# A 7x7 FFT convolution on one core: the weight copy first in the queue, the pixels behind it

## Chip, core and metric

The kernel runs on one core of one Trainium2 chip. The metric is the device time of one execution in microseconds (us). The kernel before was timed in three runs: 267.62, 270.09 and 271.57 us, median 270.09 us.

## What is computed

The reference takes an image x (1 x 224 x 224 x 96, bf16) and weights w (7 x 7 x 96 x 96, bf16), and multiplies them in the frequency domain:

```python
wp = jnp.pad(w, ((0, H - K), (0, W - K), (0, 0), (0, 0)))
Xf = jnp.fft.rfft2(x.astype(jnp.float32), axes=(1, 2))
Wf = jnp.fft.rfft2(wp.astype(jnp.float32), axes=(0, 1))
Yf = jnp.einsum('bhwi,hwio->bhwo', Xf, Wf)
y  = jnp.fft.irfft2(Yf, s=(H, W), axes=(1, 2)).astype(jnp.bfloat16)
```

The result is the cyclic 7x7 convolution of the image over 96 input and 96 output channels.

## The kernel before, in words

**Vertical direction: short transforms.** The 224 rows are cut into 8 blocks of 28 output rows (NJ, B), each seen through a window that is transformed to 17 frequencies (NS). Frequencies 0 and 16 are real, the other 15 complex, and a complex product is done with three real ones, so that each complex frequency has three weight planes ("slots"), the third being the difference of the first two (`diff`, line 390).

**Horizontal direction: taps.** The 7 horizontal taps are kept as taps, in a short fast-convolution scheme with 10 products per pair of pixels (NTAP, TAPS). The 224 columns are cut into 7 tiles t of 32 pixels.

**The stages, tile by tile.** In stage A, pixels of one image column (118 rows on the partitions: 112 rows of half an image and 6 rows of padding) are the stationary operand and the transform matrix Fm the moving one; the result goes through a PSUM bank to the buffer xf, on ScalarE or VectorE, whichever has the smaller sum of costs so far (`evac`, line 132). In stage B (`b_round`, line 556) there is one round per tile and frequency: TensorE multiplies xf and its sums and differences J (`jit`, line 526, on VectorE) by the weight planes WF, VectorE and ScalarE combine the products, and the result goes to a scratch in DRAM. Stage C transforms back with the matrix G and writes the output.

**The weights' own transform (the head).** The weights arrive as 49 rows (7 x 7 taps) of 96 x 96 numbers and have to be multiplied by the matrix Em to give WF. There are two jobs for this. The *wide jobs* (line 397) make the first 11 slots, enough for frequencies 0 to 4, in 24 jobs of four matmuls each, and read one copy of the weights, which holds all 96 output channels. The *prep jobs* (line 415) make the other slots in groups of three frequencies (PGRP) during the rounds, and read two copies of the weights at once: the second copy is shifted by 48 output channels, so that one matmul serves two channels. Both copies and Em lie in the tile wq; the first copy is at partitions 30 to 78 (W1 = 30), the second at 79 to 127, and the unused partitions 0 to 29 are zeroed, since wide jobs read partitions 0 to 78 and prep jobs all 128.

**The first two tiles are done out of order.** Tiles 0 and 1 run interleaved, tile 1 four rounds behind (LAG). Stage A of both is cut by frequency into three parts (SH2: frequencies 0 to 7, 8 to 12, 13 to 16) and by half image into two (`f_jobs`, line 511; `fj[part][half]`). A job covers 8 pixels or, in the third part, 16, and its matmuls are 64, 40 or 32 columns wide. Before, all three parts of the first half image of tile 0 are run ahead of the wide jobs (line 761); the second half's first part and the halo pixels (the six columns to the left, `a_bank`) run in the middle of the wide jobs (WMID), and J of rounds 0 to 2 is issued after the wide job 20 (JIT0). The second half's parts 1 and 2 are fillers between rounds (lines 823 and 824).

**What sets the order.** Each engine runs its instructions in program order. Fillers are put between the two halves of a round by the counter k: `add(a, b, jobs)` spreads a list of jobs over the steps a to b, two steps to a round as long as one tile runs and while both do (`pace`, line 786). The first prep jobs begin at k = 4, in the middle of round 2 (line 806). All loads and stores go through the queue of SyncE (SP), in order. Each uses one of eight semaphores in turn, so that the ninth DMA is not issued before the first has landed, and so on. Short matmuls on zeros (`warm`, line 218) keep TensorE busy while it waits for data: 14 at the start, FILL ahead of the wide jobs, one after every fourth of them.

**Constants.** Fm, Em and G are worked out on the chip: GpSimd (POOL) makes index patterns and masks (`mf` for Fm, `mk2` for Em), VectorE and ScalarE (a sine) the factors, and POOL the whole of G (`build_g`, line 340), finished by one sine and one product (`g_fin`) just ahead of round 0.

## Time and profile before

| what | value |
|---|---|
| three runs | 267.62, 270.09, 271.57 us |
| profiled execution, its own time | 269.31 us |
| its span in the profile | 267.5 us |
| TensorE (PE) busy | 255.1 us, 95% |
| VectorE (DVE) busy | 216.2 us, 81% |
| ScalarE (ACT) busy | 197.6 us, 74% |
| GpSimd (POOL) busy | 97.7 us, 37% |
| mean granted TensorE clock | 0.995 |

The span is what the profiler covers of the execution; 1.8 us of the execution's own time lie around it. All later times are counted from the start of the span. A row of the timeline gives the start, how long it lasts, engine, line, operation, the tiles written and read, the number of instructions merged into it, and in brackets the engine's idle time just before it with what ended it. PEld is the loading of the stationary operand, SPq the issue of DMAs. A row of the table of windows gives, for a stretch of time, its length, the busy time of PE, PEld, DVE, ACT and POOL (with the number of instructions that began), the granted clock, the share of time that the 16 DMA engines are busy, and GB/s.

### The profile page before, as it was taken

To read this page: it belongs to the slowest core of one execution; us is meant where nothing else is said; L and a number is where in the kernel's file an instruction comes from. 1 tells how busy PE (TensorE), PEld (TensorE's weight loads), DVE (VectorE), ACT (ScalarE), POOL (GpSimd) and SP (SyncE) were. 2 spreads that over 40 slices of the span, in tenths; PEclk is the share of its full clock that TensorE was granted. 3 is DMA by queue.
4 is the path that set the end of the run, shared out by engine and by line. 5 is a ranking of instruction groups with operands and counts; after the bars stand their busy time and mean duration, and the time that the engine had idled before them with its cause. 6 is when DMAs were issued, how large, how long until landed. Compare 5 with 4: busy or idle time off the path is not lost. (4 is left out here: it accounts for less than half of the span.)

```text
span 267.5 us, 12139 instructions
## 1 busy us (share of the span) xinstructions
PE 255.1 (95%) x5128; PEld 235.7 (88%) x5128; DVE 216.2 (81%) x465; ACT 197.6 (74%) x485; POOL 97.7 (37%) x152
## 2 busy tenths in 40 slices
PE   8897999999999999999999999999999999999983
PEld 2787999999998999999999998989999889879861
DVE  7997699889899788778887888778888789978523
ACT  8796978497964578998988789886988864187123
POOL 7771324364558344222222322233123323422100
PEclk9999999999999999999999999999999999999998
DMA  8994102711111697987876486979678443887845
GB/s 197 230 251 76 48 2 67 245 45 48 47 48 49 192 258 159 294 238 223 272 195 188 117 235 221 253 216 341 235 152 242 169 128 125 204 250 182 259 107 191
DMA packets 46690, 46.78 MB, mean 175 GB/s; under 512 B 35292, under 2 KB 38056, under 8 KB 46540
## 3 DMA queue, kind: packets, MB, share of 16 engines
q1 hardware_dynamic: 44348, 43.95, 59.6%
q10 hardware_dynamic: 2288, 2.06, 2.6%
q8 instruction: 40, 0.66, 1.1%
q14 instruction: 14, 0.11, 0.2%
HBM read 24.66 MB, written 21.33 MB: 172 GB/s over the span
## 5 line engine op out<-in xcount | busy, mean ns | idle before, releaser
L101 PE MATMUL pb<-WF,J 96*128 96x96 bf16 x2821 | 162.9, 206 | 1.7 <-DVE J L101 1.3
L101 PEld LDWEIGHTS <-J 96*128 96x128 bf16 x2821 | 138.0, 98 | 12.3 <-issue 3.5
L101 POOL TENSOR_TENSOR yf<-v,u 128x384 bf16<-128x384 f32 x79 | 81.3, 1040 | 145.7 <-issue 84.6
L101 ACT CAST xf<-pb 96x408 bf16<-96x408 f32 (+3 forms) x145 | 67.3, 486 | 7.6 <-PE pb L101 3.8
L101 PE MATMUL pb<-WF,xf 96*128 96x96 bf16 x952 | 60.0, 206 | 0.9 <-ACT WF L101 0.9
L101 DVE TENSOR_TENSOR J<-xf 96x1824 bf16<-96x1824 bf16 (+1 forms) x84 | 56.9, 716 | 0.0
L101 PEld LDWEIGHTS <-xf 96*128 96x128 bf16 x952 | 47.2, 98 | 1.3 <-issue 1.2
L101 PE MATMUL pb<-Fm,xn 118*128 118x136 bf16 (+3 forms) x640 | 45.5, 199 | 0.2 <-DVE u L101 0.2
L101 PE MATMUL pb<-tt,Gm 102*84 102x384 bf16 (+1 forms) x132 | 32.9, 326 | 0.6 <-ACT J L101 0.3
L101 PEld LDWEIGHTS <-xn 118*128 118x128 bf16 x640 | 30.3, 97 | 0.3 <-issue 0.3
L101 ACT CAST WF<-pb 96x480 bf16<-96x480 f32 (+1 forms) x58 | 28.6, 558 | 2.3 <-PE pb L101 2.3
L101 ACT CAST J<-pb 84x384 bf16<-84x384 f32 (+1 forms) x65 | 28.1, 490 | 2.6 <-PE pb L101 2.6
L101 ACT CAST yo<-pb 84x384 bf16<-84x384 f32 (+1 forms) x63 | 27.1, 486 | 2.3 <-POOL yf L101 1.3
L101 DVE TENSOR_TENSOR J<-J 96x912 bf16<-96x912 bf16 (+2 forms) x42 | 24.2, 576 | 0.0
L101 PE MATMUL pb<-wq 128*128 128x120 bf16 (+1 forms) x288 | 21.8, 226 | 0.7 <-DMA wq<-in_w_dram 0.6
L101 PEld LDWEIGHTS <-wq 128*128 128x128 bf16 (+1 forms) x288 | 19.9, 148 | 1.7 <-DVE xf L101 1.1
L101 DVE TENSOR_TENSOR yf<-v,u 128x384 bf16<-128x384 f32 x26 | 15.1, 580 | 0.9
L101 PE MATMUL pb<-wu 128*112 128x384 bf16 (+1 forms) x59 | 14.5, 391 | 1.1 <-DVE ct L101 1.1
L101 PEld LDWEIGHTS <-wu 128*112 128x112 bf16 (+1 forms) x59 | 7.4, 127 | 5.6 <-issue 3.1
L101 PEld LDWEIGHTS <-Gm 102*84 102x84 bf16 (+1 forms) x132 | 11.1, 117 | 1.0 <-issue 0.4
L101 ACT COPY xf<-xf 96x816 bf16<-96x816 bf16 (+3 forms) x20 | 11.1, 613 | 0.0
L101 ACT CAST tt<-pb 112x384 bf16<-112x384 f32 x8 | 3.6, 480 | 9.3 <-PE pb L101 9.2
(387 smaller groups left out, 239.2 us busy)
## 6 DMA issues: line engine op xcount, KB each, us to landing
scr<-yf SPq DMA_DIRECT2D x30, 288.0 KB
xn<-in_x_dram SPq DMA_DIRECT2D x12, 672.0 KB
tt<-scr SPq DMA_DIRECT2D x24, 336.0 KB
out_dram<-yo SPq DMA_DIRECT2D x12, 252.0 KB
out_dram<-J SPq DMA_DIRECT2D x12, 252.0 KB
tt<-scr SPq DMA_DIRECT2D x6, 288.0 KB
WF<-in_x_dram SPq DMA_DIRECT2D x2, 672.0 KB
out_dram<-tt SPq DMA_DIRECT2D x8, 168.0 KB
```

The costliest lines, as they stand in the source:

```text
L101: r = fn(*a, **k)
```

## The change

The change concerns the head and the first rounds; the rounds' own matmuls are the same.

- **Order of the loads.** The first weight copy is issued first, then the pixels of tile 0 (first half image), where it was the other way round.
- **Places.** The first copy goes to partitions 64 to 112 (W1 = 64), the second to 15 to 63 (W2 = 15); 15 rows are zeroed instead of 30. The wide jobs read only the 49 rows of the first copy, and 110 columns of Em instead of 128.
- **Order on PE.** 15 warm matmuls (before: 14, and 3 more behind the first pixels), then the wide jobs; part 0 of the first half image ahead of wide job 12, the halo ahead of wide job 18, part 0 of the second half after the last, then two warm matmuls, J and round 0.
- **Moved to the rounds.** Parts 1 and 2 of the first half image of tile 0 become fillers with those of the second half: part 1 over the steps 1 to 6, part 2 over 6 to 10. `diff` of frequencies 2 to 4 is one step later. The copy of tile 0's edge columns to tile 1 (`new_xf`) is issued at round 2 instead of round 1. `g_fin` moves from the head to round 3.
- **Constants.** The mask for Em is made before that for Fm, and Em's first columns before Fm. A zeroing moves from VectorE to POOL, behind `build_g`. The temporaries of `build_g` and the constant pi lie in the third J buffer. The first VectorE operation for J in round 0 is cut in two, frequency 0 first. The evacuations are dealt out as if VectorE had 900 more cost units behind it.

```diff
-FILL = 3
+FILL = 1
-WMID = 14
-JIT0 = 20
-W1 = 30
+WX0 = 12
+WHALO = 18
+W1 = 64
+W2 = 15
...
+    load_w(W1, 0, PW - 1, 0)
+    load_last(K1 - 1, 0)
     load_x(0, 0)
-    load_last(K1 - 1, 0)
-    load_w(W1, 0, PW - 1, 0)
...
-    load_w(K1, 0, PW - 1, 1)
-    load_last(EP - 1, 1)
+    load_w(W2, 0, PW - 1, 1)
+    load_last(W1 - 1, 1)
...
-    VE.memset(wz[0:W1, ZB:WE // 2], 0.0)
+    GE.memset(wz[0:W2, ZB:WE // 2], 0.0)
...
-                    TE.matmul(pv_[:, k], lhsT=wqx[0:K1, o0 + k:o0 + k + 127 * C + 1:C], rhs=ev, start=True, stop=True)
+                    TE.matmul(pv_[:, k], lhsT=wqx[W1:K1, o0 + k:o0 + k + 127 * C + 1:C], rhs=ev, start=True, stop=True)
...
+        cuts = ((0, 1), (1, n)) if t == g == 0 else ((0, n),)
...
-    for p in range(3):
-        for f in fj[p][0]:
-            f()
     warm(FILL)
+    load["v"] += 900
     for i, f in enumerate(wide_jobs()):
-        if i == WMID:
+        if i == WX0:
+            for g in fj[0][0]:
+                g()
+        if i == WHALO:
             for jg in range(2):
                 for g in a_bank(0, xf0, xh_bufs[jg], 0, 3, jg, 0):
                     g()
-            for g in fj[0][1]:
-                g()
         f()
-        if i == JIT0:
-            for g in jit(0, 0):
-                g()
         if i % FEV == FEV - 1:
             warm(1)
-    g_fin()
+    for g in fj[0][1]:
+        g()
+    warm(2)
+    for g in jit(0, 0):
+        g()
...
-                add(2 * i - 4, 2 * i - 3, [diff(i)])
-            add(1, 4, fj[1][1])
-            add(3, 7, fj[2][1])
+                add(2 * i - 3, 2 * i - 2, [diff(i)])
+            add(1, 6, fj[1][0] + fj[1][1])
+            add(6, 10, fj[2][0] + fj[2][1])
+        if r == 2:
+            new_xf(1, SH2[0], SH2[1])
...
+        if r == 3:
+            g_fin()
```

## The prediction

> **What bounds the kernel now.** I read the page first: engines, and their busy tenths in 40 slices.

> ```profile
> PE 255.1 (95%) x5128; PEld 235.7 (88%) x5128; DVE 216.2 (81%) x465; ACT 197.6 (74%) x485; POOL 97.7 (37%) x152
> ...
> PE   8897999999999999999999999999999999999983
> ```

> TensorE is the bound: nearly every slice is at nine tenths. So a time saved or lost on PE in the first 30 us goes through to the end, unless a later wait takes it. I therefore read the head in the timeline for the places where PE waits for something other than itself.

> ```profile
> 6.76 2.69 PE L101 MATMUL pb<-Fm,WF 118*128 118x64 bf16 x96 [0.35 <-DMA WF<-in_x_dram]
> ...
> 10.70 1.19 PE L101 MATMUL pb<-wq 79*128 79x128 bf16 x16 [0.60 <-DMA wq<-in_w_dram]
> ...
> 19.09 1.52 DVE L101 TENSOR_TENSOR J<-xf 96x1824 bf16<-96x1824 bf16 x2
> ...
> 20.54 0.46 DVE L101 TENSOR_TENSOR J<-J 96x608 bf16<-96x608 bf16 x1
> ...
> 20.73 0.50 PE L101 MATMUL pb<-WF,xf 96*128 96x96 bf16 x8 [0.91 <-ACT WF L101]
> ...
> 25.30 0.50 PE L101 MATMUL pb<-Fm,WF 118*128 118x32 bf16 x14 [1.23 <-issue]
> ...
> 27.20 0.81 PEld L101 LDWEIGHTS <-wq 128*128 128x128 bf16 x12 [0.25 <-DMA wq<-in_w_dram]
> ```

> The first pixels land at 6.7 us, the first weight copy at 10.7; round 0 begins at 20.73. Then a wait of 1.2 us, and at 27.20 the row that I think decides: the first prep job, in the middle of round 2, waits 0.25 us for a DMA into wq, the second weight copy. That copy is the last load of the head; whatever PE saves ahead of this point, it cannot pass it before the copy has landed. I call it the wall.

> So the third view is the DMA's rate, by windows.

> ```profile
> 5.50:8.00 2.50, 2.15 (x49) 1.47 (x48) 2.23 (x11) 2.26 (x3) 2.05 (x12) 1.00 1.01 214
> 11.00:17.00 6.00, 6.00 (x110) 5.76 (x109) 5.42 (x11) 5.44 (x12) 4.85 (x20) 1.00 1.03 260
> ...
> 20.00:26.00 6.00, 4.04 (x115) 3.96 (x115) 4.15 (x9) 3.93 (x12) 0.78 (x1) 1.00 0.55 85
> ```

> First row: the first copy alone, 214 GB/s. Second: pixels, 260. Third: the end of the second copy, 85, with the engines 55% busy. The DMA share is about 1 from 1.8 to 20 us, so loads are one queue of fixed length: its order doesn't shorten it.

> **The change, part by part.**

> *The loads.* The bytes ahead of the second copy stay the same. Only the first copy's place is new: partitions 64 to 112, where before 34 of its 49 rows were under 64. The second copy of before lies wholly at 79 to 127 and moves worse. In the trace's single DMA packets each of 16 rings has three rows of a copy in turn: a row of the first took 1.39 us on the mean; once all rings were on the second copy, a row took 1.7 to 2.4 us, about 2.0. Bounds for the new first copy: 1.39 us a row (no change) and 2.38 (the slowest row seen), so its end comes 0 to 3 x 0.99 = 3.0 us later than at the old rate. I take 2.0, the row with the nearest partitions: 3 x 0.6 = 1.8 us. All loads behind it shift by as much, the second copy too: wall 27.2 + 1.8 = 29.0. [...]

> *When the wide jobs start.* Issue at 0.8, first packet about 1.8 us as the pixels' now, three rows, and 1 us from last packet to landing as before (9.55 to 10.56): 1.8 + 4.2 + 1.0 + 0.5 for slow first packets = 7.5 at the old rate, 9.3 at the slow one. Em is ready by then: VectorE is freed of Fm (0.77) and a memset (0.90) ahead of it, and POOL makes its mask about 2.1 us sooner. The pixels land at about 10.7 + 1.8 = 12.5, and part 0 behind 12 wide jobs wants them at 9.3 + 3.6 = 12.9 (four jobs and a warm matmul take 1.21 us: 10.73 to 11.95). Thin, but on PE's order nothing behind them is urgent.

> *From the first wide job to the wall.* Wide jobs, halo and the second half's part 0 took 10.70 to 19.82 = 9.1 us; with 32 matmuls of the first half's part 0 at 2.69 / 96 = 28 ns it is 10.0. The last evacuation is 0.7, J 1.52 + 0.46 = 2.0, all now behind PE: round 1 begins 12.7 us after the first wide job, at 22.0 (20.2 at the old rate), against 22.07 before. Two full rounds' rest to the wall are 52 matmuls of 96 columns at 49 ns (1.23 us for 25) and 40 fillers at 28: 3.6 us. PE is at the wall at 25.6 (23.8) and waits for 29.0 (27.2). The head's gain, whatever it is, ends in that wait, and so does the 1.2 us wait at 25.30, even if it goes. I count the head at zero; without the wall it would be worth up to 3.4 us.

> *What is moved past the wall.* Parts 1 and 2 of the first half are 64 matmuls, and the later steps (1 to 6, 6 to 10) hold more back: in program order 398 matmuls stand ahead of the first prep job before, 326 after. These 72 now run behind the wall, on a PE that is full there: 72 x 28 ns = **2.0 us**. Their 6 evacuations (about 0.5 us each) fall on ACT and DVE, which from 27 to 39 us are busy most of the time; in program order they come with the PE work that they belong to, so I take 0; from 0 to 1.5 us (both engines full, half each).

> *At no cost.* 110 columns instead of 128 and 49 rows instead of 79: prep matmuls of 120 columns and 128 rows take the same (0.91 us for 12, against 1.19 for 16), so the width does not set it. One more J operation (0.1 us) on DVE: round 0's 8 first matmuls cover it. The memset on POOL (0.9 us on DVE; on POOL perhaps twice) comes at about 20 us; POOL's next work is at 26.8, and the prep jobs that read it are behind the wall. `g_fin`, 0.38 us on ACT and 0.78 on POOL, moves to round 3, behind POOL's sum of round 2; VectorE's write of the third J buffer waits for it, at 35.0 before; POOL is done at about 32 plus the shift. Without that cover it would cost up to 1 us. Edge copies, `diff` and cost units: moved behind or ahead of the wall wait, 0, at worst one filler, 0.6 either way. SP passes the same 18 loads; its waits for landings (eight semaphores) move to the first copy and the pixels, while the rings hold 2 us of work.

> *The sum*, against the profiled execution's own 269.31 us (span 267.5; median of the three runs 270.09, 0.8 above, inside their spread): wall +1.8, moved work +2.0 = +3.8, **273.1 us**, 1.4% slower. Bounds of this case: 0.5 to 3.0 for the wall and 0 to 1.0 on the evacuations, 271.8 to 275.3.

> **Rivals.**

> - *The copy is not slowed by its partitions.* Its rows ran evenly at 214 GB/s, near the pixels' 260, so the low rate of the second copy may be only stragglers at the end of a queue. Then the wall stays at 27.2, and 269.31 + 2.0 = **271.3** (270.8 to 271.8).
> - *The wall opens early: faster.* Place: the first prep job. If the second copy at 15 to 63 runs out as fast as the first did, with no slow end (85 GB/s), it lands at 23.8 or sooner, and PE never waits: 27.2 - 23.8 = 3.4 gained, 2.0 given back: **267.9**. It gains from a landing before 27.2 - 2.0 = 25.2 on. Against it: its rows are on one side again, and the late rings were late by the 6-row loads, which stay.
> - *The clock falls in the wait.* The warm matmuls ran 427 ns apart for about 4.3 us, then 215: PE starts at half speed. After gaps of up to 1.4 us it stayed fast; here the gap is 29.0 - 25.6 = 3.4 us. At half speed for 4.3 us it loses 2.1 us behind the wall: **275.2**. [...]

> **Chances.** Forecast 0.50, copy not slowed 0.27, faster 0.11, clock 0.12. The range holds the first two and the clock and leaves the faster case out: 269.3 to 275.6. Two per cent of the median, about what a measurement of this kernel can tell from no change, is 264.7 to 275.5: slower beyond it 0.12 (half of the clock's case, the forecast's upper end), faster 0.02, within 0.86.

> **What would show it.** Right: the first wide matmul at 8.5 to 9.5 us; PE waiting 2 to 4 us for the DMA into wq at the first prep job, at 28.5 to 30; from there to the end as long as before plus 2 us. If the wide jobs begin under 8 us, the first rival holds; if the prep job doesn't wait, the second; if 96-column matmuls behind it are about 85 ns apart, the third. It is wrong in a way not listed if PE waits in rounds 3 to 6 for ACT or DVE, or before part 0 for pixels.

## The result: 3.4% slower

The changed kernel took **278.86 us** (median of six runs, 277.65 to 279.61); the kernel before, beside it, 269.85 us. The ratio is **1.034** (95% interval 1.028 to 1.040). The prediction was 273.1 us, at most 275.6. The profiled execution took 279.61 us, its span is 277.7 us, before 267.5. Medians are over all executions of a kernel, ratios leave out those more than 1.5% above its fastest one. In the profile of the changed kernel the recording helper is line 102 instead of 101.

First the page, the rows that answer to those of before: engines, PE's tenths in 40 slices, and the clock that the chip granted to TensorE, in tenths of full speed.

```profile
PE 262.9 (95%) x5128; PEld 241.3 (87%) x5128; DVE 217.5 (78%) x465; ACT 198.8 (72%) x485; POOL 98.9 (36%) x153
...
PE   7499999999999999999999999999999999879983
...
PEclk9855799999999999999999999999999999999999
```

PE makes the same 5128 matmuls and is busy 7.8 us longer. The last row tells where: in the third to the fifth slice (14 to 35 us) the clock granted to TensorE is 0.5 to 0.7. Before it was full from 5.47 us to the tail. The timeline of PE shows the head (start, duration, tiles, form, count; in brackets the idle time before and its end).

```profile
10.68 1.48 PE L102 MATMUL pb<-wq 49*128 49x110 bf16 x16 [4.59 <-DMA WF<-in_x_dram]
12.09 0.61 PE L102 MATMUL pb<-wu 128*128 128x512 bf16 x1
12.63 1.68 PE L102 MATMUL pb<-wq 49*128 49x110 bf16 x16
...
26.57 1.91 PE L102 MATMUL pb<-Fm,WF 118*128 118x64 bf16 x32
...
29.13 0.85 PE L102 MATMUL pb<-WF,xf 96*128 96x96 bf16 x8
...
34.87 0.91 PE L102 MATMUL pb<-wq 113*128 113x120 bf16 x12
```

PE stands still for 4.59 us, then starts the wide jobs at 10.68 us, as late as before (10.70). (The releaser named in the bracket is the pixels' load; the first weight copy is what the matmul reads.) From there to round 0 at 29.13 it has no wait, and yet needs 18.45 us; before it was 10.03. Sixteen wide matmuls take 1.68 us instead of 1.19, and one matmul on zeros costs 0.54 us from its start to the next wide one (12.09 to 12.63) instead of 0.22. The first prep job, the prediction's wall, waits for nothing: it comes at 34.87 us, when the second copy has long landed. The windows of the stretch, changed kernel (length; PE, PEld, DVE, ACT, POOL busy; granted clock, DMA share, GB/s):

```profile
10.68:29.13 18.45, 18.45 (x181) 14.23 (x181) 9.95 (x16) 10.42 (x20) 8.41 (x29) 0.51 0.92 190
```

and its counterpart of before, from the first wide matmul to the end of PE's work ahead of round 0 (0.91 us of waiting follow there):

```profile
10.70:19.80 9.10, 9.10 (x146) 8.45 (x147) 8.52 (x16) 8.05 (x18) 7.03 (x26) 1.00 1.07 259
```

PE is busy without a break in both; the clock is 0.51 in the one and 1.00 in the other. The trace's clock records put the half clock at 11.20 to 31.68 us.

This is how the shift against before runs through the program. The matmuls on J come in the same order in all kernels, so the k-th of them can be compared; from PE's 680th matmul on (38.52 us before) the whole order on PE is the same.

| kernel | first wide | round 0 | first prep job | 127th J matmul, against before | 401st J matmul, against before |
|---|---|---|---|---|---|
| before | 10.70 | 20.73 | 27.23 | 0 | 0 |
| changed | 10.68 | 29.13 | 34.87 | +10.05 | +9.40 |
| place alone (experiment 9) | 12.67 | 28.76 | 35.87 | +8.65 | +8.87 |
| order alone (experiment 2) | 8.45 | 21.47 | 27.48 | +2.10 | +1.69 |
| order alone, no idle time (experiment 10) | 8.98 | 19.33 | 27.78 | +2.36 | +1.92 |

All of it is there by the 127th J matmul, at 37 to 48 us; nothing more is lost up to the last stage. There the profiled execution of the changed kernel loses 1.3 us more (+9.53 at the 2000th J matmul, +10.78 at the last); its span is 10.2 us longer than before, the median time 9.0.

### The profile page after: what moved, and what is told of

Its sections match the earlier page's. It is cut to its first block, busy times and chain, and to the rows that moved or that the text cites. A ratio compares the mean times of both kernels' runs of the same rounds, so it can differ in the third digit from the quotient of the medians.

```text
span 277.7 us, 12135 instructions
## 1 busy us (share of the span) xinstructions
PE 262.9 (95%) x5128; PEld 241.3 (87%) x5128; DVE 217.5 (78%) x465; ACT 198.8 (72%) x485; POOL 98.9 (36%) x153
## 4 chain that ended last, share of the span: by engine, by line
PE 75%; DVE 12%; DMA 7%; issue 2%; ACT 2%; DVEq 0%; ACTq 0%
PE pb L102 75%; DVE J L102 4%; DMA wq<-in_w_dram 3%; DVE v L102 3%; DVE WF L102 2%; DMA tt<-scr 1%; DVE u L102 1%; DMA scrb<-yf 1%; DVE yf L102 1%; DMA xf<-scrb 1%; ACT xf L102 1%; DVE xf L102 1%; DVE tt L102 0%; DMA WF<-in_x_dram 0%; DVEq L988 0%
## 5 line engine op out<-in xcount | busy, mean ns | idle before, releaser
L102 ACT CAST xf<-pb 96x408 bf16<-96x408 f32 (+3 forms) x146 | 68.1, 489 | 8.9 <-PE pb L102 6.8
L102 DVE TENSOR_TENSOR J<-xf 96x456 bf16<-96x456 bf16 (+3 forms) x85 | 56.8, 708 | 0.1
L102 ACT CAST WF<-pb 96x480 bf16<-96x480 f32 (+1 forms) x57 | 28.5, 563 | 9.1 <-PE pb L102 9.0
L102 ACT CAST J<-pb 84x384 bf16<-84x384 f32 (+1 forms) x64 | 27.6, 489 | 2.7 <-POOL yf L102 2.1
L102 PE MATMUL pb<-wq 113*128 113x120 bf16 (+1 forms) x288 | 24.7, 247 | 4.6 <-DMA WF<-in_x_dram 4.6
L102 PEld LDWEIGHTS <-wq 113*128 113x128 bf16 (+1 forms) x288 | 21.7, 152 | 7.1 <-issue 7.0
L102 PE MATMUL pb<-wu 128*112 128x384 bf16 (+1 forms) x59 | 15.7, 411 | 1.1 <-DVE J L102 1.1
L102 DVE CAST WF<-pb 96x440 bf16<-96x440 f32 (+1 forms) x15 | 9.3, 623 | 8.2 <-PE pb L102 7.8
```

Source lines behind the costliest of these rows:

```text
L102: r = fn(*a, **k)
```

## The experiments

**The first theories.** One: the clock fell because PE was idle for 4.6 us ahead of the wide jobs. Two: the 49 rows of the wide jobs are too few to keep the clock up, or to bring it up. Three: the order of the work is at fault and not the place. The first four runs set them apart.

### 1. A bridge over the idle time

```diff
-FILL = 1
+FILL = 22
```

> The changed kernel with 22 warm matmuls instead of 1 between the 14 first ones and the wide jobs, so that TensorE has no idle time until the first weight copy lands; all else as it is. Idle theory (the granted clock fell to half because PE idled 4.6 us ahead of the wide jobs, and the 49-row stage then could not lift it): the clock stays full in the head, the first wide job still begins at about 10.7 us, round 0 at about 21.5 instead of 29.1, the first prep job is reached at about 27 and waits some 3 us for the second copy, at about 30.3; about 274 to 275 us. Stage theory (matmuls on 49 rows bring the clock down by themselves, wait or no wait): half clock from about 3.5 us behind the first wide job, round 0 near 27 to 29, 277 to 279 us.

Measured: 276.38 us, ratio 1.018 (1.011 to 1.025). In the profiled execution, the longest of four (277.26 us), PE is busy up to the wide jobs, and the clock falls all the same, at 14.28 us instead of 11.20, for 13.7 us instead of 20.5. The page's clock row and the window from the first wide job to round 0:

```profile
PEclk9955999999999999999999999999999999999998
```

```profile
10.63:27.52 16.89, 16.89 (x180) 13.27 (x181) 9.86 (x16) 10.33 (x20) 8.44 (x29) 0.61 0.97 205
```

The idle time brings the fall forward, but here the wide stage brings it about by itself 3.6 us after it has begun. The stretch is 1.56 us shorter than in the changed kernel; 2.5 us come back in the median time. The fall does not come to the same extent each time: the four executions took 273.14, 275.99, 276.77 and 277.26 us at a mean granted clock of 0.996, 0.989, 0.974 and 0.972 (changed kernel 0.960 to 0.967, the profiled execution of before 0.995). So in one of them the clock was hardly down, and that one was 5.7 us faster than the changed kernel; why it held there stays open, for only the longest has a trace.

### 2. The order of the change in the places of before

First copy at partitions 30 to 78 again, wide jobs on 79 rows; all else as changed.

```diff
-W1 = 64
-W2 = 15
+W1 = 30
+W2 = 30
...
-                    TE.matmul(pv_[:, k], lhsT=wqx[W1:K1, o0 + k:o0 + k + 127 * C + 1:C], rhs=ev, start=True, stop=True)
+                    TE.matmul(pv_[:, k], lhsT=wqx[0:K1, o0 + k:o0 + k + 127 * C + 1:C], rhs=ev, start=True, stop=True)
```

> The changed kernel with the two copies at the places of before (partitions 30 to 78 and 79 to 127; 30 zeroed rows, the zeroing on VectorE, wide jobs on 79 rows), in the changed order of loads and jobs. Place theory (the first copy is slow because all its rows are in partitions 64 to 127): a row takes 1.4 us instead of 2.2, the first wide job begins at 8.0 to 8.7 us, the wait ahead of it is under 2.7 us and the clock stays full, the second copy lands at about 28 and PE waits for it; 271 to 273 us. Front theory (a copy that runs first, all rings at once, is slow wherever it goes): rows of 2.2 us, wide jobs at 10.5, the clock falls, 277 to 279 us.

Measured: 272.10 us, ratio 1.009 (1.005 to 1.013). In the timeline the wide jobs start 2.2 us sooner, and the wall is there:

```profile
8.45 1.38 PE L102 MATMUL pb<-wq 79*128 79x110 bf16 x16 [1.73 <-DVE wq L102]
...
27.48 0.74 PE L102 MATMUL pb<-wq 128*128 128x120 bf16 x9 [0.49 <-DMA wq<-in_w_dram]
```

In the trace's single packets a row of the first copy (18,432 B) took 1.30 us on the mean, against 1.93 (median 2.22) at partitions 64 to 112. So the place slows the copy. Most of the loss goes when the old places and with them the 79 rows come back; this run does not part the two. The clock is at half here too, from 9.06 to 15.89 us, behind an idle time of 1.73 us.

### 3. Parts 1 and 2 back in the head

Experiment 2, with the 64 moved matmuls behind the halo pixels in the head and the old steps for the second half.

```diff
+            for p in (1, 2):
+                for g in fj[p][0]:
+                    g()
...
-            add(1, 6, fj[1][0] + fj[1][1])
-            add(6, 10, fj[2][0] + fj[2][1])
+            add(1, 4, fj[1][1])
+            add(3, 7, fj[2][1])
```

> The kernel of e2_place with parts 1 and 2 of the first half image of tile 0 back in the head (behind the halo, ahead of wide job 18), and the fillers' steps as before (1 to 4 and 3 to 7). Theory (72 matmuls moved past the landing of the second copy cost 2.0 us, and ahead of it they are free): 1.5 to 2.0 us faster than e2_place, about 270. Rival (the moved work is hidden in the rounds): the same as e2_place within 0.5 us, or slower, since ahead of round 0 it costs 1.8 us.

Measured: 272.79 us, ratio 1.010 (1.004 to 1.017): no gain. The run can't be read as a test of the moved work, for PE stood still 2.29 us in the middle of a wide job, without a cause that the profile names:

```profile
8.45 1.16 PE L102 MATMUL pb<-wq 79*128 79x110 bf16 x16 [2.50 <-DVE wq L102]
...
20.97 0.42 PE L102 MATMUL pb<-wq 79*128 79x110 bf16 x3 [2.29 <-issue]
```

The clock then fell for 3.4 us, from 21.17. It had not fallen behind the 2.50 us of idle time ahead of the wide jobs (first row), more than in experiment 2. What may lie behind this stall is told below, among the unexpected; experiment 7 prices the moved work without it.

### 4. A probe of the clock

Eight stages, each on one form of matmul, most of them from a cold start. An entry of the list gives first row, end row, columns, number of matmuls, whether the stationary operand is read with a stride, and how many matmuls on 128 rows go ahead. (The list is set on fewer lines here.)

```diff
+    PH = [(0, 128, 512, 40, False, 0), (64, 113, 110, 170, True, 0), (0, 79, 128, 160, True, 0),
+          (0, 118, 64, 240, False, 0), (0, 128, 110, 170, True, 0), (0, 96, 96, 190, False, 0),
+          (64, 113, 110, 240, True, 20), (0, 49, 512, 40, False, 0)]
```

> Leaves out the convolution and writes zeros. PE runs eight stages of about 10 to 20 us, each behind an idle time of 8 us or more that lets the clock fall: matmuls on 128 rows x 512 columns; on 49 rows (partitions 64 to 112) x 110 columns with strided stationary reads as in the wide jobs; 79 rows x 128 strided; 118 x 64; 128 x 110 strided; 96 x 96; then 20 on 128 x 512 and at once 49 x 110; last 49 rows x 512. Idle theory: the 128 x 512 stage goes from 427 to about 215 ns after some 4 us; the 49 x 110 stage stays at about 92 ns to its end, since it is too little activity to lift the clock; the 79 x 128, 128 x 110 and 96 x 96 stages rise; the 49-row run behind 20 warm matmuls stays fast (50 to 62 ns). Stage theory: that run falls back to 92 ns within some 7 us. If the 49 x 110 stage rises too, neither accounts for the 20 us at half clock, and the short waits for PSUM banks between its jobs have to.

Measured, in the timeline of its PE, the stages with 49, 79, 118, 96 and again 49 rows (start, duration, form, count):

```profile
52.64 15.74 PE L64 MATMUL pb<-mv,st 49*128 49x110 bf16 x170 [7.19 <-DVE mv L56]
70.51 17.23 PE L64 MATMUL pb<-mv,st 79*128 79x128 bf16 x160 [2.13 <-DVE mv L56]
88.66 9.41 PE L64 MATMUL pb<-mv,st 118*128 118x64 bf16 x240 [0.92 <-DVE mv L56]
...
124.34 11.44 PE L64 MATMUL pb<-mv,st 96*128 96x96 bf16 x190 [5.83 <-DVE mv L56]
...
147.90 20.43 PE L64 MATMUL pb<-mv,st 49*128 49x110 bf16 x240
```

49 rows ran 92 ns apart and 79 rows 107 ns to the end of their stages, without any rise, though nothing was waited for. 118 rows went from 53 to 29 ns after 5.0 us, 96 rows from 80 to 42 after 6.9. The last of these stages, behind 20 warm matmuls on 128 rows, ran 62 ns apart for 3.8 us and then 92 to its end. A stage on 49 rows and 512 columns, not shown, ran 427 ns apart for all of its 17 us, so that it is not the number of columns. So a TensorE that is busy all the time does not get the full clock by that alone; the rows count.

### 5. The price of the clock, asked of the kernel before

```diff
-            TE.matmul(pwu[:].rearrange("p (a b) -> p a b", a=4), lhsT=wu[:, 0:128], rhs=wur, start=True, stop=True)
+            TE.matmul(pwu[:].rearrange("p (a b) -> p a b", a=4), lhsT=wu[0:49, 0:128], rhs=wur[0:49], start=True, stop=True)
```

> The kernel before, with nothing changed but the rows of its short matmuls on zeros: 49 of 128 rows (as many matmuls, 512 columns as before). If the clock goes by the rows that the matmuls use, these 20 matmuls neither lift nor hold it: the granted clock is at half from the start to past the wide jobs, the wide jobs (79 rows) run at about 107 ns a matmul instead of 62, round 0 begins some 6 us later than at 20.73 us, and PE reaches the first prep job behind the landing of the second copy at 27 us, so that the loss goes through to the end: 274 to 278 us. If only PE's being busy counts, and not its rows, nothing changes: 269 to 271 us. If the half clock is there but hidden by the wait for the second copy, it costs 0 to 2 us: 270 to 272.

Measured: 270.73 us, ratio 1.003 (0.999 to 1.008). Six executions took 269.5 to 270.9 us and make the ratio; the other four took 274.7 to 278.8 at a mean granted clock as high (0.997 to 0.999), and none of them has a trace, so what made them long stays open. In the profiled execution (270.57 us) the theory was half wrong. The 49-row matmuls did not bring the clock up: it rose at 11.34 us, behind the 118-row work, instead of 5.47. But from there the 79-row wide jobs kept it, with 118-row work only in their middle; 79 rows held a clock that was up (1.00 from 11.83 to 23.14 us), and in experiment 4 didn't raise one that was down (107 ns apart for 17 us). Round 0 came 2.4 us later than before (23.14), the first prep job 0.7 (27.96): the 4 to 8 us of the theory are not in this execution, nor in the times of the other five like it. A second thing shows in the spacing of single matmuls: around each 49-row matmul among the 79-row ones some 0.25 us are lost, though the clock is full: the wide one ahead takes 159 ns instead of 61, the 49-row one 318 instead of 220, the next wide one 114 instead of 60.

### 6. The changed kernel with the clock held

```diff
-FILL = 1
-FEV = 4
+FILL = 22
+FEV = 1
```

> The changed kernel with 22 matmuls on zeros ahead of the wide jobs, as in the bridge, and now one of them (128 rows, 512 columns) behind every wide job instead of every fourth: 18 more, 3.9 us at full clock. By the theory of rows, nearly half of the wide stage is now on 128 rows and the clock holds: no half clock from 10.7 us on, the wide stage and what follows take 10.0 + 3.9 = 14 us instead of 17 to 18, the first prep job comes at 30 to 31 us (where the second copy lands) instead of 32.5, and the time is below the bridge's 276.4, at 273 to 275 us, although more work is done. By the rival, that the clock falls for another cause than the rows of the wide matmuls, it falls all the same, the 18 matmuls cost up to 7.7 us at half clock, and the time is 280 us or more.

Measured: 279.86 us, ratio 1.041 (1.034 to 1.047), neither what the theory nor what its rival gave. The clock held, by the window from the first wide job to round 0, and the stretch took longer than ever:

```profile
10.71:30.70 19.99, 19.97 (x198) 12.78 (x198) 9.27 (x16) 10.33 (x20) 8.38 (x29) 1.00 0.84 175
```

So the half clock is not the whole of the loss. The timeline has the rest, one job after the other:

```profile
11.07 0.39 PE L102 MATMUL pb<-wu 128*128 128x512 bf16 x1
11.40 0.45 PE L102 MATMUL pb<-wq 49*128 49x110 bf16 x4
11.78 0.39 PE L102 MATMUL pb<-wu 128*128 128x512 bf16 x1
```

A job of four wide matmuls and one on zeros takes 0.71 us (11.07 to 11.78). At 62 and 216 ns each it would be 0.46. **0.25 us are lost at each change from 49 rows to 128 and back.** With this price the stretch adds up: 10.0 (the prediction's sum) + 18 more matmuls on zeros at 0.216 = 3.9, + 24 changes at 0.25 = 6.0, together 19.9; measured 19.99.

### 7. The moved work alone

The kernel before, with parts 1 and 2 of the first half image moved, and eight matmuls on zeros in their place ahead of the wide jobs. (It is the one meant by "the eighth run" in an expectation below.)

```diff
-FILL = 3
+FILL = 11
...
-    for p in range(3):
-        for f in fj[p][0]:
-            f()
+    for f in fj[0][0]:
+        f()
...
-            add(1, 4, fj[1][1])
-            add(3, 7, fj[2][1])
+            add(1, 6, fj[1][0] + fj[1][1])
+            add(6, 10, fj[2][0] + fj[2][1])
```

> The kernel before with one part of the change alone: parts 1 and 2 of the first half image of tile 0 leave the head for the steps 1 to 6 and 6 to 10; 8 more short matmuls on zeros (128 rows) take their 1.8 us ahead of the wide jobs, so that nothing else in the head moves. If the moved work is paid in full, as the prediction has it: +1.8 to +2.3 us, 271.8 to 272.5. If the waits of PE in the rounds (1.2 us at 25.3 us of before) take it up, 0 to 0.8 us: 270.0 to 270.8. If the evacuations behind the wall hold up the rounds: 273 or more.

Measured: 269.84 us, ratio 1.003 (1.000 to 1.007), against the 269.02 us of before, timed beside it. The trace tells more than the time. The first prep job came 1.08 us sooner than in the profile of before, because the second copy's packets ended sooner in this run (24.8 us against 25.8):

```profile
26.15 0.92 PE L101 MATMUL pb<-wq 128*128 128x120 bf16 x12 [0.91 <-DMA wq<-in_w_dram]
```

From there to the 127th J matmul this kernel needs 1.82 us more than before (64 x 28 ns = 1.8), to the 401st 1.2 us more: 0.6 us come back at 39 to 43 us. Experiments 2 and 10, counted from their walls, give 1.84 and 1.80, then 1.4.

### 8. An attempt at the holes of the head

```diff
-    for jg in range(2):
-        load_x(1, jg)
+    load_x(1, 0)
     load_w(K1, 0, PW - 1, 1)
     load_last(EP - 1, 1)
+    load_x(1, 1)
...
+    for f in fj[1][1]:
+        f()
     g_fin()
...
-            add(1, 4, fj[1][1])
```

> An attempt to do better from the kernel before: the second weight copy is loaded ahead of the last half image of tile 1, so that it lands some 2.6 us sooner (about 24.5 instead of 27.1 us), and part 1 of the second half image of tile 0 (0.9 us on PE) runs between the wide jobs and round 0, where PE waited 0.91 us. If the waits of the head (0.9 at 20.7, 1.2 at 25.3, 0.25 at 27.2) are what is left to gain: 1 to 2 us less, 268 to 269 us, the first prep job without a wait for a DMA. If tile 1's pixels, now last in the queue, are waited for instead: 270 to 272 us, with PE waiting for a DMA into xn at 25 to 28 us.

Measured: 271.42 us, ratio 1.007 (1.003 to 1.011). The wait for the copy and the wait at round 0 went. The time is the rival's, but not its cause: no pixels of tile 1 were waited for; a stall of 2.98 us came in the middle of a job of tile 0 whose pixels had long landed, and behind it the clock was at half from 27.11 to 30.52 us.

```profile
22.73 0.21 PE L101 MATMUL pb<-Fm,WF 118*128 118x32 bf16 x2
25.91 0.50 PE L101 MATMUL pb<-Fm,WF 118*128 118x32 bf16 x14 [2.98 <-issue]
```

### 9. The place alone

By now the theory was: the place does it, by three things, slower rows, half clock, and the loss at each change of rows. This run has the order of before and only the new places.

```diff
-W1 = 30
+W1 = 64
+W2 = 15
...
-    load_w(K1, 0, PW - 1, 1)
-    load_last(EP - 1, 1)
+    load_w(W2, 0, PW - 1, 1)
+    load_last(W1 - 1, 1)
...
-                ev = Em[0:K1, 0].rearrange("p a t -> p (a t)")[:, 0:wcol]
+                ev = Em[W1:K1, 0].rearrange("p a t -> p (a t)")[:, 0:wcol]
...
-                    TE.matmul(pv_[:, k], lhsT=wqx[0:K1, o0 + k:o0 + k + 127 * C + 1:C], rhs=ev, start=True, stop=True)
+                    TE.matmul(pv_[:, k], lhsT=wqx[W1:K1, o0 + k:o0 + k + 127 * C + 1:C], rhs=ev, start=True, stop=True)
```

> The kernel before, in its own order of loads and work, with the places alone changed as the change has them: first copy at partitions 64 to 112, second at 15 to 63, wide jobs on 49 rows and 110 columns. Theory: the 49 rows are the cause. The first copy lands some 2 us later (rows of 1.9 to 2.2 us for 1.37); each of the six or seven changes from the wide jobs to matmuls on more rows and back costs 0.25 us of empty TensorE as measured in the trace of the dense run, 1.6 us; and the clock falls by the wait ahead of the wide jobs or within 3.5 us of them and stays at half until 118-row work has run for some us, 4 to 6 us. Sum +6 to +8 us: 275 to 278 us, round 0 at 27 to 30 us instead of 20.7. Rival, that the place acts by the loads alone: +2 to +2.5 us, 271 to 272.5 us. Rival, that the order of the change is the cause: 269 to 270.5 us.

Measured: **278.18 us, ratio 1.034 (1.030 to 1.038)**, the same as the whole change. The timeline:

```profile
12.67 1.21 PE L102 MATMUL pb<-wq 49*128 49x110 bf16 x16 [2.40 <-DMA wq<-in_w_dram]
13.81 0.61 PE L102 MATMUL pb<-wu 128*128 128x512 bf16 x1
14.35 1.69 PE L102 MATMUL pb<-wq 49*128 49x110 bf16 x16
...
28.76 0.80 PE L102 MATMUL pb<-WF,xf 96*128 96x96 bf16 x8 [0.25 <-ACT WF L102]
```

The first copy lands 2 us later (12.67 for 10.70), the first 16 matmuls still run fast, the clock falls at 13.65 and is back at 34.13, round 0 comes 8 us late. The place, with the 49 rows that come with it, is the cause, whatever the order; the 110 columns are not, for experiments 2 and 10 have them too.

### 10. The order alone, without idle time

Experiment 2 with a bridge: does the head's gain end in the wait for the second copy, as predicted?

```diff
-FILL = 1
+FILL = 12
```

> The changed order in the places of before (the second experiment), with 12 matmuls on zeros instead of one ahead of the wide jobs, so that TensorE has no idle time of 2 us there. Theory: in the second experiment the clock fell because of that idle time, and 79 rows hold a clock that is up: no half clock now, round 0 at 18 to 19.5 us instead of 21.5. What that gains ends in the wait for the second copy: the first prep job still begins at 27 to 27.6 us, now after 2 to 3 us of waiting, and the time stays at 271 to 272.5 us. Rival, that no wall stands there and the head's gain goes through: 269 to 270 us. Rival, that 79 rows do not hold the clock: it falls at 12 to 13 us all the same, and the time is 272 us or more.

Measured: 271.26 us, ratio 1.010 (1.006 to 1.014). No half clock, and the window from the first wide job to round 0 is what the prediction had for the changed kernel:

```profile
8.98:19.33 10.35, 10.32 (x182) 9.27 (x180) 8.76 (x16) 9.35 (x20) 8.15 (x33) 1.00 1.07 244
```

and the timeline has a matmul on zeros between wide jobs at 0.21 us, and the wall:

```profile
9.95 0.38 PE L102 MATMUL pb<-wu 128*128 128x512 bf16 x1
10.16 1.13 PE L102 MATMUL pb<-wq 79*128 79x110 bf16 x16
...
27.78 0.90 PE L102 MATMUL pb<-wq 128*128 128x120 bf16 x12 [2.94 <-DMA wq<-in_w_dram]
```

PE is ready for the prep job 3 us before the copy (2.94 by the bracket, which counts from a modelled end; 3.15 from start to start of the matmuls, 3.1 of it waiting). Against experiment 2 the head is 2.1 us faster at round 0, and the time is the same (intervals 1.006 to 1.014 and 1.005 to 1.013). The wall is shown.

### 11. A second attempt

Experiment 7, with the second copy ahead of tile 1's last half image, and part 1 of the first half image run between the wide jobs and round 0.

```diff
-    for jg in range(2):
-        load_x(1, jg)
+    load_x(1, 0)
     load_w(K1, 0, PW - 1, 1)
     load_last(EP - 1, 1)
+    load_x(1, 1)
...
+    for f in fj[1][0]:
+        f()
     g_fin()
...
-            add(1, 6, fj[1][0] + fj[1][1])
+            add(1, 6, fj[1][1])
```

> An attempt to do better: the kernel before with parts 1 and 2 of the first half image moved to the rounds (as in the eighth run), the second weight copy loaded ahead of the last half image of tile 1, and part 1 of the first half image run between the wide jobs and round 0, where PE waited 1.08 us. If the wait of 1.1 us for the second copy and that at round 0 go, and no stall without a named cause comes at 22 to 26 us: 1 to 2 us less than before, 267.0 to 268.5 us. If such a stall comes, as in the last attempt (3 us there): 269 to 271 us.

Measured: 269.19 us, ratio 0.999 (0.996 to 1.002): no difference from before. The wall is gone, and a stall without a cause came again, here ahead of round 0 and 1.29 us long. No version was found that beats the kernel before.

### 12. A probe of the change of rows

An entry of the list gives first row, end row, columns, number of matmuls, after how many of them one on 128 rows and 512 columns follows (0: never), how many of those go ahead, and whether a pause follows these. (The list is set on fewer lines here.)

```diff
+    PH = [(0, 79, 128, 200, 0, 20, False), (0, 79, 128, 160, 16, 0, False), (64, 113, 110, 160, 16, 20, False),
+          (64, 113, 110, 120, 4, 20, False), (0, 64, 110, 96, 16, 20, False), (0, 65, 110, 96, 16, 20, False),
+          (0, 79, 128, 160, 0, 20, True)]
```

> A probe of TensorE alone: it leaves out the whole convolution and writes zeros. Seven stages of matmuls, after long pauses. Stages on 49 rows (partitions 64 to 112) with one matmul of 128 rows and 512 columns after every 16 or every 4; the same on 64 and on 65 rows; 79 rows without any other, with one 128-row matmul after every 16 from cold, and after a pause of 2.5 us. If a change between matmuls on at most 64 rows and on more empties the array, the 128-row matmul with what lies around it takes 0.25 us more on 49 and on 64 rows, and nothing more on 65 and 79. If it is the number of rows left idle or the place, 64 and 65 rows are alike. For the clock: if 79 rows hold a clock that is up, the first stage stays at full for its 13 us; if a pause of 2.5 us takes it down, the last one goes to half; if every 16th matmul on 128 rows is not enough to hold it on 49 rows, that stage falls to half within 7 us, and every 4th holds it.

Measured, in the timeline of its PE: 16 matmuls on 64 rows, then one on 128, and the same on 65 rows.

```profile
145.27 1.19 PE L69 MATMUL pb<-mw,st 64*128 64x110 bf16 x16
146.39 0.39 PE L71 MATMUL pb<-mv,st 128*128 128x512 bf16 x1
146.71 1.18 PE L69 MATMUL pb<-mw,st 64*128 64x110 bf16 x16
...
165.94 1.13 PE L69 MATMUL pb<-mw,st 65*128 65x110 bf16 x16
166.91 0.38 PE L71 MATMUL pb<-mv,st 128*128 128x512 bf16 x1
167.13 1.15 PE L69 MATMUL pb<-mw,st 65*128 65x110 bf16 x16
```

A period is 1.44 us on 64 rows (145.27 to 146.71) and 1.19 on 65 (165.94 to 167.13). One row more, and the 0.25 us are gone. In the single matmuls: the last on 64 rows 157 ns instead of 62, the one on 128 rows 322 instead of 216 to 220, the next about 40 more; the same on 49 rows; nothing on 65. At half clock, on 49 rows, the loss is 0.26 us, 0.14 of it on the last matmul ahead of the change. The edge lies between 64 and 65 rows; the place is not it, for the 49 rows were at partitions 64 to 112 and the 64 at 0 to 63.

For the clock, the windows of five stages (length; PE, PEld, DVE, POOL busy; clock, DMA share, GB/s): 79 rows alone from a full clock; 79 rows from cold with every 17th matmul on 128 rows; 49 rows with every 17th; 49 rows with every 5th; 64 rows with every 17th.

```profile
41.78:54.10 12.32, 12.32 (x200) 12.32 (x199) 9.94 (x3) 0.00 (x0) 1.00 0.01 3
62.83:83.69 20.86, 20.86 (x169) 18.51 (x169) 14.26 (x3) 0.00 (x0) 0.50 0.00 1
92.32:110.52 18.20, 18.20 (x170) 13.79 (x170) 9.18 (x2) 0.00 (x0) 0.65 0.00 1
117.69:138.35 20.66, 20.66 (x150) 12.32 (x150) 10.61 (x2) 0.00 (x0) 1.00 0.00 1
143.87:152.20 8.33, 8.33 (x103) 6.84 (x102) 6.56 (x2) 0.00 (x0) 1.00 0.01 2
```

79 rows hold the clock for 12 us and don't raise it in 21. 49 rows lose it (at 97.71, 5.4 us after their start) with one matmul of 17 on 128 rows, as in the wide jobs, and keep it with one of 5; 64 rows with one of 17 keep it for the 8.3 us of their stage. The pause of 2.5 us, in the last stage, did not come about in the run, so that what idle time does to 79 rows rests on experiments 2, 3 and 10.

## Why the prediction was wrong

**The step that failed is "At no cost": "110 columns instead of 128 and 49 rows instead of 79".** It held the matmuls of before against each other, all on more than 64 rows; the trace of before has none on fewer. The 49 rows cost two things, which the runs set apart. The same order on 79 rows with a full clock takes 10.35 us from the first wide job to round 0 (experiment 10), on 49 rows 18.45: 8.1 us more.

- *The changes of rows.* Between the wide jobs stand five matmuls on zeros, one of them with part 0, and the halo; with the last matmul on zeros and the second half's part 0 behind the wide jobs, that is six changes there and back and a last one there. By the prices at half clock of experiment 12 they cost 6 x 0.26 + 0.14 = 1.7 us.
- *The half clock.* The rest of the 8.1, 6.4 us, and 0.4 more up to the first prep job (5.74 us from round 0 against 5.34, waits aside): 6.8 us. This figure is a remainder and not measured by itself. Two runs bear it out: in experiment 6, with a full clock and 24 changes, the stretch adds up without any other loss, and the one execution of experiment 1 whose clock was hardly down was 5.7 us faster than the changed kernel.

What TensorE does at such a change no run shows. Measured is its price, 0.25 us for the way there and back, and its edge, between 64 rows (1.44 us a period in experiment 12) and 65 (1.19). The prediction weighed no cost of that kind.

**On the path** the first prep job is 34.87 us against 27.78 in experiment 10: +1.7 for the first copy's later landing (first wide job 10.68 against 8.98), +1.7 and +6.8 for the two losses, -3.1 for the wait that is no longer there, 7.1 in all. Experiment 10 itself reaches the wall 0.56 us later than the kernel before, and the moved work costs 1.4 us more past the wall: 7.1 + 0.56 + 1.4 = 9.05 us at the 401st J matmul. Measured are +9.40, so that 0.35 us have no name, and 278.86 - 269.85 = 9.0 in the time.

Point by point:

- **"The loads"**: right in kind, a little too small. A row of the first copy took 1.93 us on the mean, with 2.0 taken, but 2.22 at the median, with 2.38 as the bound; its long rows needed 1.84 to 8.88 = 7.0 us from first to last packet, against 4.8 in experiment 2: 2.2 later, with 1.8 forecast. The second copy's last long row ended at 29.35 us, before at 25.83: 3.5 later, with 1.8 forecast. It cost nothing in the end, for PE came later still. Why the rows at partitions 64 to 112 took longer no run shows.
- **"When the wide jobs start"**: 10.68 us, forecast 9.3. The last packet, a short piece of the 49th row, ended 0.7 us later than forecast (9.01 against 8.3), and 1.7 us instead of 1.0 went by from there to the first wide job.
- **"From the first wide job to the wall"**: 10.0 us for the head's PE work, measured 18.45; on 79 rows the sum was good (10.35, and round 1 12.4 us after the first wide job, forecast 12.7).
- **The wall**: it held up nothing in the changed kernel, for PE came later than the copy; shown in experiments 2 and 10. By the prediction's own signs, a first prep job that does not wait would have spoken for the wall opening early; it can also mean, as here, that PE is late. That a gain of the head ends there was right: 2.1 us of it in experiment 10 moved nothing.
- **"What is moved past the wall"**: 2.0 us, measured 1.8 behind the wall and 1.2 to 1.4 for good. The six evacuations cost nothing that shows. The zeroing that moved from VectorE to POOL took 0.93 us there (at 19.94 us), and not twice the 0.90 of before.
- **The rivals.** The copy not slowed: refuted by the rows. The wall opening early: the copy landed later, not sooner. "The clock falls in the wait" had the right agent in the wrong place, at the wall and for 2.1 us; that a gap of 3.4 us takes the clock down no run had shown. The place to look was in the prediction's own numbers: the matmuls on zeros end at about 6 us, the wide jobs were to begin at 9.3. PE had 3.3 us of idle time there, as much as the 3.4 us at the wall that were weighed, ahead of a stage on 49 rows, which in experiment 4 never brought the clock back. It fell at 11.20 us; in the profiled execution of experiment 1, without that gap, at 14.28 us.

In the places of before the prediction would have been a fair one: its sum without the 1.8 us for the copy is 271.3 us, and the order alone gave 271.3 to 272.1. In part that is luck, for the moved work cost less than forecast (1.4 of 2.0 us for good) and the wall came 0.3 to 0.6 us later.

**What idle time does to the clock** can be read from the twelve traces of whole kernels together. The granted clock changed only at steps of 3.41 us: 9.06 - 5.65 in experiment 2, and every spell between two changes is a whole multiple of it. In the head it fell at the end of each step in which PE, by its modelled ends, had been idle for 1.73 us or more (1.73, 2.22, 2.29, 2.40 and 2.89 in experiments 2, 8, 3, 9 and the changed kernel) and held through all with 1.70 us or less, but for the wide stage on 49 rows in experiment 1, where it fell without any. The bound is not sharp: one step with 1.82 us, late in experiment 1, held. Experiment 3 has a longer gap ahead of the wide jobs than experiment 2, 2.50 us against 1.73, but a step ends in the middle of it, at 7.52 us (1.57 us before, 0.93 behind), and the clock held. So the place of a gap among the steps seems to count as well as its length; no run moved a gap by itself to try it. For the wall the prediction weighed a gap of 3.4 us; here 1.73 us of idle time in a step of 3.41, half of it, were enough.

## What to carry to other kernels

Before a matmul is cut to fewer rows, look at which side of 64 it ends on, and with what it alternates: on 49 and on 64 rows each trip to a matmul on 128 rows and back cost 0.25 us here, on 65 rows nothing, which made the cheap matmuls on zeros between jobs dearer than the jobs. A stage that is busy is not a stage that holds the clock: read the granted clock together with the rows in use, and ask of every stage that is put first whether it could bring the clock back (79 rows could not in 17 us, 49 rows not in 16). And when a change mixes a place and an order, run each alone first; here the place alone was 8.3 us and the order alone 1.4 to 2.1.

## What had not been expected of the hardware

**TensorE seems to wait for its own instructions.** The stalls without a cause (1.23 us at 25.30 us of before, 2.29 in experiment 3, 2.98 in experiment 8, 1.29 in experiment 11) stand behind the 348th, 221st, 348th and 220th matmul of the trace: two places, 127 to 128 matmuls apart. One of the trace's two DMA queues for instructions brings 16,384 B at a time; on the page of before it has 40 packets (0.66 MB), and PE 5128 matmuls with a weight load each: 128 matmuls to a packet, if all of them are PE's. In each case a packet of that size ended during the stall or up to 0.5 us ahead of it: at 23.97, 19.50, 24.53 and 19.54 us, with PE running again 1.3 to 1.8 us later. Most kernels pass the same two places without a stall, and the times tell them apart: in all twelve traces PE ran on freely where it reached the place 1.77 us or more after the end of its packet (up to 7.6 us), and stood still wherever it came sooner, the four times above and twice for a moment (0.1 us in experiment 8 at the 220th matmul, 1.6 us after the packet; 0.3 us in experiment 11 at the 348th, 1.0 us after). The longest stall was 2.98 us. The agreement of places and times is what speaks for a wait for instructions; no run moved one of the two places by itself, so it is argued and not shown. It would explain why filling the holes of the head (experiments 8 and 11) gained nothing: PE would have come to the place before its instructions did.
